# Attention and spectral mixing in one kernel: values loaded in fp32 by SyncE, and their bf16 copies shared by GpSimd and VectorE

## The chip, the core and the metric

The kernel runs on one core of a Trainium2 chip. The time is what the device needs for one execution of the whole program, in microseconds. Sixteen runs of the kernel before took 455.35 to 459.65 us, with a median of 456.8 us. The engines are named as in the profile: PE is TensorE (matrix products), DVE is VectorE, ACT is ScalarE, POOL is GpSimd, SP is SyncE, which here only starts transfers. GpSimd starts transfers too, and only its transfers convert fp32 to bf16 on the way.

## The reference

Two operations follow one another. The first is causal attention in a window of 128 positions with a linear bias, for 8 batches, 8 heads, 576 positions and 64 channels a head; the second multiplies the lowest 64 Fourier modes of the sequence by complex matrices of 512 x 512 each.

```python
scores = scale * np.matmul(q, k.transpose(0, 1, 3, 2))
bias = slopes[:, None, None] * (-np.abs(rel))[None, :, :]
mask = (rel >= 0) & (rel < 128)
attn = softmax(np.where(mask, scores + bias[None], -1e9))
x = np.matmul(attn, v).transpose(0, 2, 1, 3).reshape(B, S, H * D)

X = np.fft.rfft(x, axis=1)
Yr = einsum('bmd,mde->bme', Xr, w_r) - einsum('bmd,mde->bme', Xi, w_i)
Yi = einsum('bmd,mde->bme', Xr, w_i) + einsum('bmd,mde->bme', Xi, w_r)
y = np.fft.irfft(Y, n=S, axis=1)          # Y is 0 above mode 64
u = x + y
return u + np.maximum(u @ w_ch, 0.0)
```

All inputs are fp32 in memory. The mode matrices are the bulk: 128 of them (64 real, 64 imaginary) of 1.05 MB each, of which the imaginary one of mode 0 isn't needed.

## The kernel before

**Attention** works on 16 units, a unit being one batch and four heads. The order of all work is written by hand: the list `STAGE` names some 23 steps with a lag each, and stage s runs each step for unit s minus its lag, so that loads, casts, transposes, scores, exponentials, products with the values and normalisation of several units are under way at once. An engine runs its own instructions strictly in the order in which this list issues them; so does each queue of transfers.

For a unit, `load` brings queries (one transfer, 2304-byte runs), keys (per pair of heads a main part of 512 positions and a tail of 64, both tails into the lower 64 partitions, `L230`) and values (main `L216` and tail `L220`). Queries and keys are started by SyncE as fp32. Values are started by GpSimd and arrive as bf16. Every raw buffer is double: `cast` of unit u ends with `load` of unit u+2 into the same place, which waits for the cast.

`cast` turns raw data into what TensorE takes. For q and k it is one VectorE instruction that converts to bf16 and interleaves the heads (`L259`). For v it is eight instructions, one for each of four quarters of 32 partitions (n) and each of two alternating positions (a): quarter (n, a) goes to the 32 partitions that start at 64 (n % 2) + 32 a of the buffer `vb` (`L252`), beside columns of ones from which the row sums come; a ninth copies the tail into `vt` (`L255`). The eight wait until the value products of unit u-2 have left the same `vb` buffer. In a stage VectorE's order is: values of unit s, keys of unit s+2, `norm` (reciprocal and product, `L380`, `L381`) of unit s-1's first two heads, queries of unit s+3, two mask products (`L339`), `norm` of the other two heads. `value` (`L365`) writes one PSUM buffer, so the second product of a unit waits for the first `norm`.

Key tails of both head pairs lie in partitions 0 to 63, and two transposes of 64 rows handle them (`L282`); the unused upper half is set to zero once (`L500`).

**Weights before their time.** While attention runs, GpSimd starts some mode matrices as bf16: `AHEAD` says how many after which stage, into a pool of `EARLY` tiles, and a one-element copy (`gate`, `L562`) from the first normalised result of the unit before holds each back to its stage. `LATER` does the same into raw buffers that attention no longer needs (the list `spare`). GpSimd's queue is thus, in each stage: values of unit s+2 (two transfers), gate, one weight.

**Spectral part.** After attention TensorE multiplies mode after mode (`L870`); weights that were not brought early stream in as fp32, started by SyncE, into six tiles (`NWA`) in the space that attention leaves, and eight more (`AGAIN`) as bf16 into early tiles that have been used. Projections, inverse transform and output follow from there.

Of the kernel before, what the change touches and what calls it, by code (L numbers as in the profile page):

```python
# [10 lines left out]
FP32 = mybir.dt.float32  # L11
BF16 = mybir.dt.bfloat16
# [8 lines left out]
P = 128  # L21
D = 64
# [5 lines left out]
FULL = 4  # L28
TAIL = 64

TPP = 9

W = D + 2

NC = 24


STAGE = (
# [68 lines left out]
class _Attention:  # L107
# [100 lines left out]
    def load(self, w, u):  # L208
        nc = self.nc
        if u >= len(self.units):  # L210
            return
        b, g = self.units[u]
        hs = slice(4 * g, 4 * g + 4)
        if w == "v":
            t = self.raw["v"][:, u % 2], self.raw["t"][64:96, u % 2]
            nc.gpsimd.dma_start(  # L216
                out=t[0],
                in_=self.v[b, hs, : FULL * P].rearrange("h (p j) d -> p h (j d)", j=4),
            )
            nc.gpsimd.dma_start(  # L220
                out=t[1],
                in_=self.v[b, hs, FULL * P :].rearrange("h (p j) d -> p h (j d)", j=2),
            )
        elif w == "k":
            t = self.raw[w][:, u % 2]
            for e in range(2):
                src = self.k[b, 4 * g + 2 * e : 4 * g + 2 * e + 2]
                for row, j0, n, part in ((slice(0, P), 0, 8, src[:, : FULL * P]),
                                         (slice(0, 64), 8, 2, src[:, FULL * P :])):
                    nc.sync.dma_start(  # L230
                        out=t[row, e, j0 : j0 + n].rearrange("p j d -> p (j d)"),
                        in_=part.rearrange("h (p j) d -> p h (j d)", j=n),
                    )
        else:
            t = self.raw[w][:, u % 2]
            nc.sync.dma_start(
                out=t.rearrange("p e j d -> p e (j d)"),
                in_=self.q[b, hs].rearrange("(e h) (p j) d -> (h p) e (j d)", h=2, j=TPP),
            )
        self.loaded[w, u] = t  # L240

    def cast(self, u, w):

        nc = self.nc
        src = self.loaded.pop((w, u))
        if w == "v":
            rows = src[0].rearrange("p h (j a d) -> p h j a d", j=2, a=2)
            for n in range(4):
                c0 = W * (n % 2)
                for a in range(2):  # L250
                    r = 64 * (n % 2) + 32 * a
                    nc.vector.tensor_copy(  # L252
                        self.vb[u % 2][r : r + 32, n // 2, :, :, c0 : c0 + D],
                        rows[32 * n : 32 * n + 32, :, :, a])
            nc.vector.tensor_copy(self.vt[u % 2][64:96, :, :, :D],  # L255
                                  src[1].rearrange("p h (j d) -> p h j d", j=2))
        else:
            dst = self.mid.tile([P, src.shape[2], 2, D], BF16, tag=w, name=w)
            nc.vector.tensor_copy(dst.rearrange("p j e d -> p e j d"), src)  # L259
            self.casted[u, w] = dst  # L260
        self.load(w, u + 2)

    def transpose(self, u, w):
        nc = self.nc
        src = self.casted.pop((u, w))
        tag = dict(tag="sc", bufs=2) if (u, w) == (0, "k") else dict(tag="tp")
        tp = self.ps.tile([P, TPP * P], BF16, name="tp", **tag)
        self.open[w, u] = tp
        if w == "q":
            for j in range(TPP):  # L270
                nc.tensor.transpose(tp[:, j * P : (j + 1) * P],
                                    src[:, j].rearrange("p e d -> p (e d)"), self.ident)
            return
        main = tp[:, : FULL * 2 * P].rearrange(
            "d (h j b a i p) -> d j a i h b p", h=2, j=2, b=FULL, a=2, p=16, i=2)
        rest = tp[:, FULL * 2 * P :].rearrange("d (j h i p) -> d j h i p", j=2, h=2, i=2)
        for j in range(8):
            nc.tensor.transpose(
                main[:, j // 2 % 2, j % 2, j // 4], src[:, j].rearrange("p e d -> p (e d)"),
                self.ident.rearrange("k (b p h) -> k h b p", b=FULL, h=2))  # L280
        for j in range(2):
            nc.tensor.transpose(  # L282
                rest[:, j], src[:64, 8 + j].rearrange("p e d -> p (e d)"),
                self.ident[:64, :64].rearrange("k (p i h) -> k h i p", i=2, h=2))

    def evacuate(self, u, w):
        tp = self.open.pop((w, u))
# [123 lines left out]
    def channels(self, u, _):  # L411
# [3 lines left out]
        if g < self.NG - 1:  # L415
            return
        xt = self.open.pop(("xt", u))
        NM = self.F.shape[2] // 2
        view = self.XC[:, : 4 * NC * NM].rearrange(
            "p (q s t b m) -> p q t s b m", q=2, s=3, t=2, b=8)[:, :, :, :, b]  # L420
# [13 lines left out]
def kernel(  # L434
# [10 lines left out]
    nc = tc.nc  # L445
    ctx.enter_context(tc.manual_schedule(engines=ALL | {SP}))
    B, H, S, _ = q.shape
    NM, DM, _ = moe_w_r.shape
    AHEAD = {0: 1, 1: 1, 2: 1, 3: 1, 4: 1, 5: 1, 7: 1, 8: 1, 9: 1, 10: 1, 11: 1, 12: 1, 13: 3}
    LATER = {14: 3, 15: 2}  # L450
    EARLY, NWA, NWB, AGAIN = 15, 6, 2, 8
    HM = NM // 2

    const = ctx.enter_context(tc.tile_pool(name="const", bufs=1))
    x = const.tile([P, B, FULL + 1, DM], BF16, name="x")
    XC = const.tile([P, 4 * NC * NM + 16 * NM], BF16, name="XC")
    ident = const.tile([P, P], BF16, name="ident")
# [7 lines left out]
        tc.tile_pool(name="w1", bufs=EARLY, side="right", reuse_waits="tile")  # L465
    )
    rawpool = actx1.enter_context(tc.tile_pool(name="raw", bufs=1, side="right"))
    raw = {w: rawpool.tile([P, 2, 2, n, D], FP32, name=w + "r") for w, n in (("q", TPP), ("k", 10))}
    raw["v"] = rawpool.tile([P, 2, 4, 4 * D], BF16, name="vr")
    raw["t"] = rawpool.tile([P, 2, 4, 2 * D], BF16, name="vtr")  # L470
    spare = [raw[w][:, i].rearrange("p e j d -> p (e j d)") for w in "qk" for i in range(2)]
    spare = [t[:, : 2 * DM].bitcast(BF16) for t in spare]
    spare.append(raw["v"].rearrange("p u h d -> p (u h d)"))
    spare = [t.rearrange("p (a e) -> p a e", a=4) for t in spare]
    wq, homes, todo_w, again = {}, {}, [0, *range(2, 2 * NM)], []

    def load_w(n, pool, bf16, chosen=None):


        for i in ([i for i in todo_w if i not in again][:n] if chosen is None else chosen):  # L480
            todo_w.remove(i)
            src = (moe_w_r, moe_w_i)[i % 2][i // 2].rearrange("(p a) e -> p a e", a=4)
            homes[i] = pool
            if bf16:
                t = spare.pop(0) if pool is None else pool.tile([P, 4, DM], BF16, tag="w", name="w")
                nc.gpsimd.dma_start(out=t, in_=src)
                wq[i] = [t[:, a] for a in range(4)]
            else:
                t = pool.tile([P, 4, DM], FP32, tag="w", name="w")
                for part in ((slice(0, 4),) if i < 2 * NM - 1  # L490
                             else (slice(0, 2), slice(2, 3), slice(3, 4))):
                    nc.sync.dma_start(out=t[:, part], in_=src[:, part])
                wq[i] = [t[:, a].bitcast(BF16)[:, 1::2] for a in range(4)]

    with ExitStack() as actx:
        at = _Attention(tc, actx, q, k, v, (ident, F, FT), x, XC, raw)
        n = len(at.units)
        for w, u in (("q", 0), ("k", 0), ("q", 1), ("k", 1)):
            at.load(w, u)
        nc.vector.memset(raw["k"][64:, :, :, 8:], 0.0)  # L500
        done = set()

        def run(name, arg, u):
            if 0 <= u < n and (name, arg, u) not in done:
                done.add((name, arg, u))
                getattr(at, name)(u, arg)
# [10 lines left out]
        for t in at.kT:  # L517
            nc.vector.memset(t[:, 2 * S :], 0.0)
        at.distances(pool)
        at.load("v", 0)  # L520
        at.fixtures(0)
        next(table, None)
        at.load("v", 1)
        at.fixtures(1)
        nc.gpsimd.memset(XC[:, 4 * NC * NM :], 0.0)
        run("cast", "q", 0)
# [23 lines left out]
        for stage in range(min(lags), n + max(lags)):  # L550
            for name, arg, lag in STAGE:
                run(name, arg, stage - lag)
                if name in ("transpose", "exp") and side.get(stage):
                    for _ in range(1 + (name == "transpose")):
                        fn, h = side[stage].pop(0)
                        fn(h)
            if stage == 3:
                at.inverse_table()
            if stage in AHEAD:
                if stage:  # L560
                    b, g = at.units[stage - 1]
                    nc.gpsimd.tensor_copy(gate[:1, :1], x[:1, b, 0, 256 * g : 256 * g + 1])  # L562
                load_w(AHEAD[stage], early, True)
            if stage in LATER:
                load_w(LATER[stage], None, True)

    with ExitStack() as mctx:
# [273 lines left out]
        for g in range(NM // 4):  # L841
# [5 lines left out]
            for i in range(8):  # L847
# [3 lines left out]
                w = wq[2 * m + ri]  # L851
# [13 lines left out]
                for a in range(4):  # L865
                    c0 = (a // 2 * 2 * NC + 16 * (1 - ri) + a % 2 * 8) * NM + m
                    window.append(XC[:, c0 : c0 + 31 * NM + 1 : NM])
# [9 lines left out]
                k = 8 * g + i  # L877
# [4 lines left out]
                if k == K1 - 1:  # L882
# [15 lines left out]
                    for b in range(2):  # L898
                        nc.gpsimd.dma_start(
                            out=FM.rearrange("(k v) b s -> k v b s", v=16)[:, b, b],  # L900
# [103 lines left out]
```

The softmax here doesn't subtract the row's maximum and nothing guards it: scores larger than these inputs give would overflow.

## Time and profile before

| | |
|---|---|
| median of 16 runs | 456.8 us (455.35 to 459.65) |
| the profiled execution | 458.43 us, of which the span from first to last instruction 456.5 us |
| mean granted TensorE clock | 0.890 |
| busy: PE, DVE, ACT, POOL | 366.7, 192.6, 152.9, 102.9 us |
| transfers from SyncE's queue | 132.17 MB, 73.0% of 16 engines' span |
| transfers from GpSimd's queue | 20.17 MB (as written), 26.2% |
| read from memory, written to it | 162.53 MB, 9.44 MB |
| first and last exponential of attention | 11.5 us, 136.9 us |
| first product with a mode's weights | 145.56 us |
| value copies on VectorE (`L252`) | 128, median 284 ns, at most 1058 ns |

In the profile a line such as `L252 DVE COPY vb<-vr 32x512 bf16<-32x512 bf16 x8` names the source line, the engine, the operation, what is written from what, the shapes (partitions x elements) and how many there were. In a listing in order of time, the first two numbers are the start and the length in us, and a bracket at the end says how long the engine had stood idle before, and for whom. Transfer rates in GB/s count bytes as they are written, so a transfer that converts fp32 to bf16 counts half of what it reads.

### The profile page before, as it was taken

Reading aid. Unit: us, or ns where it says so; the run is one execution under the profiler, and the core shown is the slowest. Engines: PE = TensorE matmul, PEld = TensorE weight load, DVE = VectorE, ACT = ScalarE, POOL = GpSimd, SP = SyncE. Lnnn points to the kernel's source line nnn. Section 1 sums busy time; section 2 is a strip of 40 time slices with the busy share of each in tenths; the row PEclk is TensorE's granted clock in tenths of the full one; section 3 lists DMA queues with packets and bytes.
Section 4 is the critical chain, followed back from the end, with each engine's and each line's share of the span. In section 5 each row is a group of like instructions: output and inputs, shape, how many; then the busy total and the mean of one; then the engine's idle time right before and its main releaser. Section 6 shows DMA issues by size and latency. Waiting matters only on the chain. (4 is left out here: it accounts for less than half of the span.)

```text
span 456.5 us, 8161 instructions
## 1 busy us (share of the span) xinstructions
PE 366.7 (80%) x3330; PEld 192.6 (42%) x3330; DVE 192.6 (42%) x420; ACT 152.9 (33%) x196; POOL 102.9 (23%) x170
## 2 busy tenths in 40 slices
PE   4588898899996876567665776999999999776994
PEld 3256576766664431222222233444444443332331
DVE  6889889999994210010101023121212112220584
ACT  4758798888881000000000011112111210110772
POOL 8943323242521300200000000000000000054781
PEclk8659899999998885775667699999999999999998
DMA  7999999999899999999999999999999999997598
GB/s 261 206 252 265 269 227 238 241 269 278 131 192 275 316 315 314 327 373 427 419 420 423 422 422 419 420 420 419 422 420 419 423 417 421 420 406 247 188 351 300
DMA packets 47625, 152.85 MB, mean 335 GB/s; under 512 B 7252, under 2 KB 18276, under 8 KB 35044
## 3 DMA queue, kind: packets, MB, share of 16 engines
q1 hardware_dynamic: 31156, 132.17, 73.0%
q0 software_dynamic: 16432, 20.17, 26.2%
q8 instruction: 26, 0.43, 0.4%
q14 instruction: 11, 0.09, 0.1%
HBM read 162.53 MB, written 9.44 MB: 377 GB/s over the span
## 5 line engine op out<-in xcount | busy, mean ns | idle before, releaser
L870 PE MATMUL acc<-w,XC 128*32 128x512 bf16 x464 | 136.4, 458 | 47.3 <-DMA w<-in_moe_w_r_dram 28.0
L870 PEld LDWEIGHTS <-XC 128*32 128x32 bf16 x508 | 60.2, 140 | 124.0 <-issue 88.0
L329 ACT ACTIVATE att<-sc 128x1024 bf16<-128x1024 f32 x64 | 64.0, 1031 | 8.3 <-PE sc L320 8.3
L655 POOL DMA_DIRECT2D Z<-yq x19 | 9.7, 518 | 215.2 <-issue 208.6
L642 ACT CAST ZW<-zw 128x512 bf16<-128x512 f32 x8 | 4.7, 585 | 157.5 <-PE zw L640 157.5
L614 DVE TENSOR_SCALAR yq<-acc 128x512 bf16<-128x512 f32 x13 | 9.0, 689 | 97.0 <-PE acc L870 96.9
L365 PE MATMUL av<-vb,att 128*128 128x132 bf16 (+1 forms) x576 | 38.7, 218 | 9.6 <-DVE x L381 6.8
L717 ACT CAST XW<-my 128x512 bf16<-128x512 f32 x36 | 19.3, 589 | 75.5 <-PE my L665 75.5
L365 PEld LDWEIGHTS <-att 128*128 128x128 bf16 x704 | 36.9, 99 | 15.5 <-DVE x L381 11.7
L689 DVE COPY xT<-tr 128x1024 bf16<-128x1024 bf16 x18 | 12.5, 692 | 69.8 <-PE tr L687 69.8
L252 DVE COPY vb<-vr 32x512 bf16<-32x512 bf16 x128 | 38.1, 298 | 2.3 <-DMA vr<-in_v_dram 0.8
L708 PE MATMUL my<-wch,xT 128*64 128x512 bf16 x288 | 34.5, 382 | 0.8 <-DVE xT L689 0.8
L216 POOL DMA_DIRECT2D vr<-in_v_dram x16 | 17.9, 1118 | 60.3 <-DVE vb L252 60.3
L320 PE MATMUL sc<-qT,kT 64*64 64x256 bf16 (+2 forms) x640 | 25.7, 269 | 3.0 <-ACT kT L289 2.4
L381 DVE TENSOR_TENSOR x<-av,rec 128x640 bf16<-128x640 f32 x32 | 26.4, 825 | 1.1
L822 DVE TENSOR_TENSOR o<-yy,r 128x512 f32<-128x512 f32 (+1 forms) x24 | 21.7, 953 | 6.4 <-ACT r L779 4.7
L320 PEld LDWEIGHTS <-kT 64*64 64x64 bf16 x640 | 14.8, 111 | 20.5 <-issue 16.4
L708 PEld LDWEIGHTS <-xT 128*64 128x64 bf16 x288 | 14.8, 109 | 18.9 <-issue 6.9
L307 PE MATMUL sc<-bias,ident 128*128 128x512 bf16 x64 | 20.9, 411 | 1.2 <-ACT att L329 1.0
L644 DVE CAST Z<-z 64x512 bf16<-64x512 f32 x16 | 11.0, 689 | 23.7 <-PE z L637 23.6
L779 ACT ACTIVATE r<-mm 128x512 f32<-128x512 f32 (+1 forms) x24 | 18.1, 812 | 7.5 <-PE mm L665 4.2
L339 DVE TENSOR_TENSOR att<-att,mask 128x1024 bf16<-128x1024 bf16 x32 | 20.6, 684 | 0.0
(140 smaller groups left out, 414.5 us busy)
## 6 DMA issues: line engine op xcount, KB each, us to landing
w<-in_moe_w_r_dram SPq DMA_DIRECT2D x53, 1024.0 KB, 18.4
w<-in_moe_w_i_dram SPq DMA_DIRECT2D x45, 1024.0 KB, 18.1
qr<-in_q_dram SPq DMA_DIRECT2D x16, 576.0 KB, 8.3
kr<-in_k_dram SPq DMA_DIRECT2D x32, 256.0 KB, 6.1
w<-in_moe_w_i_dram POOLq DMA_DIRECT2D x15, 512.0 KB, 12.0
out_dram<-o SPq DMA_DIRECT2D x10, 512.0 KB, 3.7
vr<-in_v_dram POOLq DMA_DIRECT2D x16, 256.0 KB, 6.8
w<-in_moe_w_r_dram POOLq DMA_DIRECT2D x8, 512.0 KB, 8.8
```

Of the source, the lines that this page charges most:

```text
L252: nc.vector.tensor_copy(self.vb[u % 2][r : r + 32, n // 2, :, :, c0 : c0 + D], rows[32 * n : 32 * n + 32, :, :, a])
L307: nc.tensor.matmul(sc[:, e], lhsT=self.ident, rhs=self.bias[self.units[u][1]][:, 2 * e + h].rearrange("p j n -> p (j n)"), start=True, sto ...
L320: nc.tensor.matmul(sc[64 * half : 64 * half + 64, e, j * 256 + c0 : j * 256 + c0 + n], lhsT=kT[row, k0 : k0 + 64], rhs=qT[row, h, q0 : q0 ...
L329: self.nc.scalar.activation(self.att[u % 2][:, kt * 8 * P : (kt + 1) * 8 * P], sc.rearrange("p e n -> p (e n)"), AF.Exp, scale=1.0 / math. ...
L339: nc.vector.tensor_tensor(out=rows, in0=rows, in1=self.table[g][:, t % 2 :: 2], op=ALU.mult)
L365: nc.tensor.matmul(bank[:, qt * W : qt * W + rhs[j].shape[1]], lhsT=att[:, o : o + P], rhs=rhs[j], start=(n == 0 and j == 0), stop=(n == l ...
L381: nc.vector.tensor_tensor(out=self.x[:, b, :, cs].rearrange("p t (h d) -> p h t d", h=2), in0=tiles[:, :, :, :D], in1=rec.unsqueeze(-1).br ...
L708: nc.tensor.matmul(mm[ROWS[half]], lhsT=lhsT, rhs=wch[:, dt], start=(dt == 0), stop=False, skip_group_check=True,)
L717: nc.scalar.copy(XW[:, j, n], mms[n])
L779: nc.scalar.activation(r[:, c], mm[:, c], AF.Relu)
L822: nc.vector.tensor_tensor(out=o[:, c], in0=yy[:, c], in1=r[:, c], op=ALU.add)
L870: nc.tensor.matmul(into[32 * (i // 2) : 32 * (i // 2) + 32], lhsT=window[a], rhs=w[a], start=(ri == 0 and a == 0), stop=(ri == (m > 0) and ...
```

## The change

Values are loaded by SyncE instead of GpSimd, as fp32: the raw buffers for values double in size, each read being 1 KB (tail: 512 bytes). The conversion to bf16 thus moves into `cast`: of the eight shifted quarter copies the first five (in the order of the loops) are made by GpSimd, three and the tail by VectorE. The values of the first two units are requested right after the queries and keys of the first two units, ahead of the tables' setup.

The raw key buffer is laid out anew: both head pairs' main parts first, then 128 columns for the tails, the tail of the first pair in partitions 0 to 63 and that of the second in 64 to 127. The key cast becomes two instructions, the tail transposes four instead of two, and the setting to zero goes.

The memory for this comes from the early weights: `EARLY` is 14 instead of 15 and stage 3 asks for none. In return there are seven spare raw buffers instead of five, and `LATER` fills four instead of two in stage 15.

```diff
+NPOOL = 5
...
         if w == "v":
             t = self.raw["v"][:, u % 2], self.raw["t"][64:96, u % 2]
-            nc.gpsimd.dma_start(
+            nc.sync.dma_start(
                 out=t[0],
                 in_=self.v[b, hs, : FULL * P].rearrange("h (p j) d -> p h (j d)", j=4),
             )
-            nc.gpsimd.dma_start(
+            nc.sync.dma_start(
                 out=t[1],
...
-                for row, j0, n, part in ((slice(0, P), 0, 8, src[:, : FULL * P]),
-                                         (slice(0, 64), 8, 2, src[:, FULL * P :])):
+                for row, c0, n, part in ((slice(0, P), 512 * e, 8, src[:, : FULL * P]),
+                                         (slice(64 * e, 64 * e + 64), 1024, 2,
+                                          src[:, FULL * P :])):
...
-                    nc.vector.tensor_copy(
+                    (nc.gpsimd if 2 * n + a < NPOOL else nc.vector).tensor_copy(
                         self.vb[u % 2][r : r + 32, n // 2, :, :, c0 : c0 + D],
                         rows[32 * n : 32 * n + 32, :, :, a])
...
-            dst = self.mid.tile([P, src.shape[2], 2, D], BF16, tag=w, name=w)
-            nc.vector.tensor_copy(dst.rearrange("p j e d -> p e j d"), src)
+            dst = self.mid.tile([P, TPP, 2, D], BF16, tag=w, name=w)
+            if w == "q":
+                nc.vector.tensor_copy(dst.rearrange("p j e d -> p e j d"), src)
+            else:
+                nc.vector.tensor_copy(dst[:, :8].rearrange("p j e d -> p e j d"),
+                                      src[:, : 16 * D].rearrange("p (e j d) -> p e j d", e=2, j=8))
+                nc.vector.tensor_copy(dst[:, 8].rearrange("p e d -> p (e d)"), src[:, 16 * D :])
...
         for j in range(2):
-            nc.tensor.transpose(
-                rest[:, j], src[:64, 8 + j].rearrange("p e d -> p (e d)"),
-                self.ident[:64, :64].rearrange("k (p i h) -> k h i p", i=2, h=2))
+            for e in range(2):
+                row = slice(64 * e, 64 * e + 64)
+                nc.tensor.transpose(
+                    rest[row, j], src[row, 8, j],
+                    self.ident[row, row].rearrange("k (p i h) -> k h i p", i=2, h=2))
...
-    AHEAD = {0: 1, 1: 1, 2: 1, 3: 1, 4: 1, 5: 1, 7: 1, 8: 1, 9: 1, 10: 1, 11: 1, 12: 1, 13: 3}
-    LATER = {14: 3, 15: 2}
-    EARLY, NWA, NWB, AGAIN = 15, 6, 2, 8
+    AHEAD = {0: 1, 1: 1, 2: 1, 4: 1, 5: 1, 7: 1, 8: 1, 9: 1, 10: 1, 11: 1, 12: 1, 13: 3}
+    LATER = {14: 3, 15: 4}
+    EARLY, NWA, NWB, AGAIN = 14, 6, 2, 8
...
-    raw["v"] = rawpool.tile([P, 2, 4, 4 * D], BF16, name="vr")
-    raw["t"] = rawpool.tile([P, 2, 4, 2 * D], BF16, name="vtr")
+    raw["v"] = rawpool.tile([P, 2, 4, 4 * D], FP32, name="vr")
+    raw["t"] = rawpool.tile([P, 2, 4, 2 * D], FP32, name="vtr")
...
-        for w, u in (("q", 0), ("k", 0), ("q", 1), ("k", 1)):
+        for w, u in (("q", 0), ("k", 0), ("q", 1), ("k", 1), ("v", 0), ("v", 1)):
             at.load(w, u)
-        nc.vector.memset(raw["k"][64:, :, :, 8:], 0.0)
...
         at.distances(pool)
-        at.load("v", 0)
         at.fixtures(0)
         next(table, None)
-        at.load("v", 1)
         at.fixtures(1)
```

More of the change, by code (lines that the diff above doesn't have):

```diff
@@ L227, in load @@
                 src = self.k[b, 4 * g + 2 * e : 4 * g + 2 * e + 2]
-                for row, j0, n, part in ((slice(0, P), 0, 8, src[:, : FULL * P]),
-                                         (slice(0, 64), 8, 2, src[:, FULL * P :])):
+                for row, c0, n, part in ((slice(0, P), 512 * e, 8, src[:, : FULL * P]),
+                                         (slice(64 * e, 64 * e + 64), 1024, 2,
+                                          src[:, FULL * P :])):
                     nc.sync.dma_start(
-                        out=t[row, e, j0 : j0 + n].rearrange("p j d -> p (j d)"),
+                        out=t[row, c0 : c0 + n * D],
                         in_=part.rearrange("h (p j) d -> p h (j d)", j=n),
@@ L467 @@
     rawpool = actx1.enter_context(tc.tile_pool(name="raw", bufs=1, side="right"))
-    raw = {w: rawpool.tile([P, 2, 2, n, D], FP32, name=w + "r") for w, n in (("q", TPP), ("k", 10))}
-    raw["v"] = rawpool.tile([P, 2, 4, 4 * D], BF16, name="vr")
-    raw["t"] = rawpool.tile([P, 2, 4, 2 * D], BF16, name="vtr")
[L471 to L474, printed above, removed]
+    raw = {"q": rawpool.tile([P, 2, 2, TPP, D], FP32, name="qr"),
+           "k": rawpool.tile([P, 2, 2 * TPP * D], FP32, name="kr")}
+    raw["v"] = rawpool.tile([P, 2, 4, 4 * D], FP32, name="vr")
+    raw["t"] = rawpool.tile([P, 2, 4, 2 * D], FP32, name="vtr")
+    spare = [raw["q"][:, i].rearrange("p e j d -> p (e j d)") for i in range(2)]
+    spare += [raw["k"][:, i] for i in range(2)]
+    spare += [raw["v"][:, i].rearrange("p h d -> p (h d)") for i in range(2)]
+    spare.append(raw["t"].rearrange("p u h d -> p (u h d)"))
+    spare = [t[:, : 2 * DM].bitcast(BF16).rearrange("p (a e) -> p a e", a=4) for t in spare]
     wq, homes, todo_w, again = {}, {}, [0, *range(2, 2 * NM)], []
```

## The prediction

> **What bounds the kernel now.** I read the table of busy slices first, then sums over three stretches, then one stage of VectorE in order of time.
>
> ```profile
> DVE  6889889999994210010101023121212112220584
> DMA  7999999999899999999999999999999999997598
> GB/s 261 206 252 265 269 227 238 241 269 278 131 192 275 316 315 314 327 373 427 419 420 423 422 422 419 420 420 419 422 420 419 423 417 421 420 406 247 188 351 300
> ```
>
> One slice is 11.4 us. VectorE is full in the first twelve slices (attention) and nearly idle after; from slice 18 on the DMA engines move a steady 420 GB/s of fp32 weights. So the kernel has two halves with different bounds.
>
> ```profile
> core 0: us, PE busy (x) PEld busy (x) DVE busy (x) ACT busy (x) POOL busy (x), PEclk, DMA share, GB/s
> 30.00:124.00 94.00, 84.46 (x1472) 62.53 (x1470) 87.65 (x209) 79.84 (x88) 33.54 (x49) 0.97 1.07 244
> 124.00:140.00 16.00, 14.01 (x253) 10.67 (x251) 13.37 (x34) 11.69 (x14) 4.42 (x9) 1.00 1.06 192
> 140.00:400.00 260.00, 209.18 (x1170) 92.83 (x1168) 42.48 (x97) 23.98 (x45) 8.88 (x20) 0.86 1.02 397
> ```
>
> In 30 to 124 us VectorE works 87.65 of 94 us, TensorE 84.46, ScalarE 79.84. Bytes are counted as written, and a casting load reads twice what it writes, so 192 GB/s there is not a slack link: at 124 us seven casting weight loads are issued at once, 1.05 MB read each. From then on transfers never pause until the last weights near 417 us: 115 of the 127 weights and w_ch are still to be read, 121.6 MB, and 121.6 MB / 420 GB/s = 289.5 us, so 124 + 289.5 = 413.5 us. The end is therefore set by two things: when that burst starts (behind attention stage 13, so by VectorE's pace) and how many weights are in before it.
>
> One stage of VectorE:
>
> ```profile
> 89.27 2.37 DVE L252 COPY vb<-vr 32x512 bf16<-32x512 bf16 x8
> 91.67 0.28 DVE L255 COPY vt<-vtr 32x512 bf16<-32x512 bf16 x1
> 91.99 0.83 DVE L259 CAST k<-kr 128x1280 bf16<-128x1280 f32 x1
> 92.73 0.21 DVE L380 RECIPROCAL rec<-av 128x10 f32<-128x10 f32 x1
> 92.98 0.82 DVE L381 TENSOR_TENSOR x<-av,rec 128x640 bf16<-128x640 f32 x1
> 93.72 0.75 DVE L259 CAST q<-qr 128x1152 bf16<-128x1152 f32 x1
> 94.39 1.29 DVE L339 TENSOR_TENSOR att<-att,mask 128x1024 bf16<-128x1024 bf16 x2
> 95.59 0.21 DVE L380 RECIPROCAL rec<-av 128x10 f32<-128x10 f32 x1
> 95.84 0.82 DVE L381 TENSOR_TENSOR x<-av,rec 128x640 bf16<-128x640 f32 x1
> ```
>
> No row has idle time in front of it; the next eight copies start at 96.58, so a stage is 7.31 us of gapless VectorE work.
>
> Last, what happens where GpSimd and VectorE work in the same microsecond, at start-up and at one mask (each line is an instruction, start and duration):
>
> ```profile
> 17.84 1.01 POOL L141 MEMSET vb<- 64x1056 bf16 x1
> 17.95 1.05 DVE L252 COPY vb<-vr 32x512 bf16<-32x512 bf16 x1
> ...
> 19.11 1.12 POOL L141 MEMSET vb<- 64x1056 bf16 x1
> 19.32 1.06 DVE L252 COPY vb<-vr 32x512 bf16<-32x512 bf16 x1
> ...
> 123.41 1.28 DVE L339 TENSOR_TENSOR att<-att,mask 128x1024 bf16<-128x1024 bf16 x2
> 123.62 0.51 POOL L562 COPY gate<-x 1x1 bf16<-1x1 bf16 x1 [0.27 <-DVE x L381]
> ```
>
> A copy that takes 0.28 us alone took 1.05 and 1.06 us beside a memset, both times ending 0.15 us after it (18.85 to 19.00, 20.23 to 20.38). In reverse, a one-element GpSimd copy took 0.51 us and ended 0.04 us after the first mask product (123.41 + 0.68, its mean on the page, = 124.09; 123.62 + 0.51 = 124.13). The two engines take turns. The PSUM-to-SBUF copy of queries at 13.19 us took 1.36 us beside memsets and 1.34 us away from them: work that reads PSUM is not held.
>
> **The change, part by part, for one unit of attention.**
>
> VectorE work. Five of eight copies go: start to start they are 2.40/8 = 0.30 us, so -1.50. The three that stay read fp32. The fp32 tensor_scalar rows at start-up (128x320 0.326 us, 128x640 0.497) give 0.53 ns an element and 0.43 us at 512, against 0.284: three times +0.145 = +0.44, and vt +0.145. (The k and q casts, 0.827 at 1280 and 0.750 at 1152, would give 0.37; that is the lower bound, 0.25 us less over four copies.) The k cast becomes 128x1024 (0.70) plus 128x128 (0.22) in place of 0.83: +0.10. Sum -1.50 + 0.44 + 0.145 + 0.10 = -0.82 us a unit if GpSimd were elsewhere.
>
> GpSimd work. A 64x512 bf16 copy at 8.66 us, with no lock in the way, took 0.603 us, 64x384 took 0.505: I take 0.60 for a 32x512 one. No row has GpSimd reading fp32 at this width or writing to other partitions than it reads, which several of these copies do; the dearest near row is the select of 32x256 from fp32 at 0.613, so 1.2 us at 512 is the upper bound; 0.5 (the 384 row) the lower. I take 0.60, for the operation is the same, a copy. Five are 3.0 us of a 7 us stage; the two load issues that leave its queue (1.18 + 0.56 us) were no load on VectorE. GpSimd itself has room: the price is the turns.
>
> The turns. The copies of unit u+1 are freed when value(u-1, 1) ends, since that unit's vb buffer is then free. That product starts after norm 0 and ends at 95.35 us in the stage shown, 0.24 us before the second reciprocal. So two GpSimd copies fit beside reciprocal and norm 1 (PSUM work, 1.0 us, free). Copies 3, 4 and 5 meet VectorE's next work: its own three vb copies and vt. A blocked VectorE copy ends 0.15 us after its blocker at 512 bf16, where it needs some 0.13 us of streaming, so its fixed part is hidden; an fp32 one needs 0.27. A blocked GpSimd operation lost only 0.05 us of its own (memset 1.12 us, of which 0.20 waiting, against 0.97). One pair is then 0.55 + 0.27 = 0.82 us where VectorE alone needs 0.44: +0.38, three times +1.14 us.
>
> By row, -0.82 + 1.14 = +0.32 us a unit. Units 0 to 13 lie ahead of the burst: 14 x 0.32 = +4.5 us.
>
> The Trainium skill ("SBUF — State Buffer", section "SBUF: two separate sides") says that the pair of ports which VectorE and GpSimd share is an exclusive lock, held for the whole instruction. The rows above agree on who waits, but not on the price: with whole instructions in line a pair would cost 0.60 + 0.43 = 1.03 us, +0.59 a pair, +0.95 us a unit and +13 us in place of +4.5. I keep to the rows.
>
> Weights before the burst. The first list loses its stage 3 entry, 12 to 11 weights by stage 12, the pool goes from 15 to 14 tiles; the two spares more are filled inside the saturated stretch. One weight of 1.05 MB joins the 289.5 us: +2.5 us. Its place in the attention stretch is not a bottleneck that gains from its absence, for VectorE sets the pace there.
>
> At nothing I cost: the value loads on the wire (same bytes read; 0.29 MB more written in 7.7 us, 38 GB/s on 244, below 420); SyncE's two more issues a unit, between a weight's 0.35 and a key load's 0.78 us (four in 3.12), so at most 1.6 on 3.7 us of a 7.3 us stage; the two more key transposes (two took 0.27 us; TensorE has 9.5 idle of 94 us, and uncovered they would cost 14 x 0.27 = 3.8); the kr memset (0.48 us at 0.91, before the first data).
>
> New waits. On SyncE, the load of v(u+2) waits for the slower engine's copies of v(u), with k(u+4) and q(u+5) queued behind; VectorE's vt ends last in the turns above, so it adds nothing in a steady stage. At start-up, q of unit 4 was issued near 21.8 us and would come behind v2 near 24 us; with 8.3 us to landing it arrives near 33 us, where it is cast at 30.7: up to 1.5 us. The memsets move up by the 2.1 us of two load issues and meet the bias products; against that the 0.77 us wait for v0 and two blocked copies (0.77 each) go. Start-up: 0, bounds -1.5 and +1.5.
>
> Sum: +4.5 + 2.5 + 0 = +7.0 us. The profiled execution took 458.43 us (span 456.5), 1.6 above the median of 456.8; the change is set on the median: 463.8 us.
>
> **Rivals.**
>
> A. GpSimd's copies are longer. At 0.85 us, VectorE's first copy waits 0.45 us and three pairs cost +0.63 each: 2.3 in place of 1.14, +1.5 a unit, 14 x 1.5 + 2.5 = +23, 480 us. At the bound of 1.2 us it is +3.3 a unit, 505 us. For it: fp32 in, other partitions out, no row. Against: the same operation at 0.60.
>
> B. Faster: the turns cost little, because GpSimd's copies fall beside PSUM work or VectorE's gaps. It decides from below 0.64 us a unit, for (0.82 - 0.64) x 14 = 2.5. With one collision left (0.38): -0.44 x 14 + 2.5 = -3.7, 453 us; with none -9, 448 us, and there TensorE (84.46 of 94 us, 6.9 us a stage) is the next bound, equal to 7.72 - 0.82. For it: norm and reciprocal are 2 us of each stage. Against: the copies are freed just ahead of VectorE's own.
>
> C. No change: the turns cost near 0.64 us, and the two halves cancel.
>
> **How the numbers follow.** Forecast 0.47 (its own range 460 to 469, one pair more or less, start-up's bounds with it), A 0.24, B 0.22, C 0.07. A measurement of this kernel tells about 0.2%, 0.9 us. Slower 0.71, same 0.07, faster 0.22. For 8 in 10 I leave out A above 480 (about 0.13) and B below 451 (0.05): 451 to 480.
>
> **What would show it.** Right: VectorE's fp32 vb copies at 0.43 us or, blocked, 0.7 to 0.85; stages near 7.6 us; GpSimd copies of 0.6 to 0.9 us; the first of the clustered weight loads at 127 to 129 us rather than 124; 420 GB/s after it as before. Wrong: GpSimd copies over 0.85 us alone (A); VectorE's copies unblocked and stages under 7.1 us (B); or value products waiting for GpSimd's copies, or VectorE idle before q or k casts for late loads, which I hold for absent.

## The result, and the profile after

The changed kernel takes 462.49 us (median of 9 runs, 461.45 to 465.16) against 456.49 us for the kernel before (48 runs by then): a ratio of 1.013, with a 95% interval of 1.0109 to 1.0151, or +5.9 us. The forecast was +7.0 us and 463.8 us. The profiled execution took 462.23 us, its span 460.2 us; that of the kernel before lay about 2 us above its median, so the two spans stand only 3.7 us apart, and below whole kernels are compared by ratios, profiles only by stages.

Part of those 2 us can be seen in the profile of the kernel before: the granted TensorE clock falls to half (0.50, third from the end), and VectorE stands idle for a product of TensorE.

```profile
54.00:56.00 2.00, 2.00 (x23) 1.29 (x22) 2.00 (x4) 0.89 (x1) 1.06 (x2) 0.50 1.10 331
```
```profile
58.26 0.22 DVE L380 RECIPROCAL rec<-av 128x10 f32<-128x10 f32 x1 [1.71 <-PE av L365]
```

The other profiles have such stretches too, at other times; over the first 47 us the mean granted clock is 0.85 in the changed kernel. Comparisons of single profiles outside the steady stages are therefore rough.

The busy slices and the sums over three stretches of the changed kernel:

```profile
DVE  6888999999995210000101033121212122220594
DMA  8879999999899999999999999999999999997498
GB/s 258 257 240 310 286 279 265 277 288 301 205 197 262 318 315 317 315 336 387 424 422 420 422 419 422 419 422 419 422 419 419 421 420 422 419 408 269 169 352 310
```
```profile
30.00:124.00 94.00, 81.77 (x1468) 61.50 (x1458) 88.11 (x159) 77.38 (x85) 54.03 (x80) 0.98 1.01 284
124.00:140.00 16.00, 15.01 (x269) 11.02 (x269) 14.98 (x27) 13.75 (x17) 12.57 (x21) 1.00 0.91 190
140.00:400.00 260.00, 205.90 (x1181) 92.52 (x1177) 43.22 (x99) 23.81 (x45) 8.75 (x20) 0.87 1.02 391
```

The picture is the same: VectorE full in attention (88.11 of 94 us, with 159 instructions where there were 209), then transfers at 420 GB/s. Values in fp32 raised what is written in attention from 244 to 284 GB/s, and from 20 us on no VectorE instruction waits for a value load. GpSimd went from 33.5 to 54.0 us.

One stage of VectorE, in order of time:

```profile
98.94 1.92 DVE L256 CAST vb<-vr 32x512 bf16<-32x512 f32 x3
100.89 0.71 DVE L259 CAST vt<-vtr 32x512 bf16<-32x512 f32 x1
101.63 0.69 DVE L266 CAST k<-kr 128x1024 bf16<-128x1024 f32 x1
102.24 0.22 DVE L268 CAST k<-kr 128x128 bf16<-128x128 f32 x1
102.38 0.21 DVE L391 RECIPROCAL rec<-av 128x10 f32<-128x10 f32 x1
102.62 0.82 DVE L392 TENSOR_TENSOR x<-av,rec 128x640 bf16<-128x640 f32 x1
103.37 0.75 DVE L264 CAST q<-qr 128x1152 bf16<-128x1152 f32 x1
104.03 1.29 DVE L350 TENSOR_TENSOR att<-att,mask 128x1024 bf16<-128x1024 bf16 x2
105.23 0.22 DVE L391 RECIPROCAL rec<-av 128x10 f32<-128x10 f32 x1
105.48 0.82 DVE L392 TENSOR_TENSOR x<-av,rec 128x640 bf16<-128x640 f32 x1
106.34 0.42 DVE L256 CAST vb<-vr 32x512 bf16<-32x512 f32 x1
```

The stage is 7.40 us (98.94 to 106.34) and again without a gap. Three copies and vt take 2.69 us of it, where nine took 2.72 us before. Why four are now as dear as nine were stands in the same microseconds of both engines:

```profile
98.43 0.60 POOL L256 CAST vb<-vr 32x512 bf16<-32x512 f32 x1
98.94 0.42 DVE L256 CAST vb<-vr 32x512 bf16<-32x512 f32 x1
99.07 0.75 POOL L256 CAST vb<-vr 32x512 bf16<-32x512 f32 x1
99.37 0.74 DVE L256 CAST vb<-vr 32x512 bf16<-32x512 f32 x1
99.87 0.71 POOL L256 CAST vb<-vr 32x512 bf16<-32x512 f32 x1
100.12 0.74 DVE L256 CAST vb<-vr 32x512 bf16<-32x512 f32 x1
100.63 0.69 POOL L256 CAST vb<-vr 32x512 bf16<-32x512 f32 x1
```

The copy at 98.43, beside a norm that reads PSUM, takes GpSimd 0.60 us, and VectorE's first takes 0.42: neither was held. From there they take turns, one of each every 0.75 us. Over all units the page has a mean of 666 ns for VectorE's copies and 738 for GpSimd's:

```profile
L256 POOL CAST vb<-vr 32x512 bf16<-32x512 f32 x80 | 59.1, 738 | 15.6 <-issue 10.1
...
L256 DVE CAST vb<-vr 32x512 bf16<-32x512 f32 x48 | 31.9, 666 | 0.9
```

As the measure of a stage I take the start of the vt copy, unit 5 to unit 13, eight stages: before 61.98 to 121.36 us, 7.42 us a stage; after 63.37 to 123.80, 7.55 us. The burst of weight loads starts at 126.65 us instead of 124.09.

### The profile page after: what moved, and what is told of

Its sections match the earlier page's. It is cut to its first block, busy times and chain, and to the rows that moved or that the text cites. A ratio compares the mean times of both kernels' runs of the same rounds, so it can differ in the third digit from the quotient of the medians.

```text
span 460.2 us, 8284 instructions
## 1 busy us (share of the span) xinstructions
PE 365.4 (79%) x3362; PEld 193.5 (42%) x3362; DVE 197.0 (43%) x355; ACT 152.7 (33%) x196; POOL 134.0 (29%) x218
## 5 line engine op out<-in xcount | busy, mean ns | idle before, releaser
L880 PE MATMUL acc<-w,XC 128*32 128x512 bf16 x456 | 131.7, 451 | 45.1 <-DMA w<-in_moe_w_r_dram 26.2
L256 POOL CAST vb<-vr 32x512 bf16<-32x512 f32 x80 | 59.1, 738 | 15.6 <-issue 10.1
L256 DVE CAST vb<-vr 32x512 bf16<-32x512 f32 x48 | 31.9, 666 | 0.9
L350 DVE TENSOR_TENSOR att<-att,mask 128x1024 bf16<-128x1024 bf16 x32 | 22.2, 735 | 0.0
```

The lines of the kernel that those rows point to most:

```text
L256: (nc.gpsimd if 2 * n + a < NPOOL else nc.vector).tensor_copy(self.vb[u % 2][r : r + 32, n // 2, :, :, c0 : c0 + D], rows[32 * n : 32 * n ...
L350: nc.vector.tensor_tensor(out=rows, in0=rows, in1=self.table[g][:, t % 2 :: 2], op=ALU.mult)
L880: nc.tensor.matmul(into[32 * (i // 2) : 32 * (i // 2) + 32], lhsT=window[a], rhs=w[a], start=(ri == 0 and a == 0), stop=(ri == (m > 0) and ...
```

## The experiments

Times below are ratios to runs of the kernel before on the same chip; "steady stage" is the measure just named.

**The turns taken away.** GpSimd's five copies are left out from the third unit on; later units find the values of the first two in those rows.

```diff
                 for a in range(2):
+                    if u >= 2 and 2 * n + a < NPOOL:
+                        continue
                     r = 64 * (n % 2) + 32 * a
```

> The changed kernel with GpSimd's five copies left out from the third unit on (those units use the values of the first two in these rows, so the output is not the reference's). If the turns cost VectorE about 0.95 us a unit: stage 7.45 - 0.95 = 6.5, below TensorE's 6.9, so -0.55 x 12 = -6.6 us, 456 us, and every VectorE value copy at 0.42 us. If the loss lies elsewhere (transfers, start-up, the early weight): 462 us, no change.

Measured: 455.21 us, ratio 0.996 (0.9937 to 0.9982); steady stage 6.97 us. VectorE's stage and the sums over 60 to 116 us, of this kernel and then of the changed one (columns: PE, PEld, DVE, ACT, POOL busy):

```profile
93.28 0.82 DVE L394 TENSOR_TENSOR x<-av,rec 128x640 bf16<-128x640 f32 x1
94.14 1.29 DVE L258 CAST vb<-vr 32x512 bf16<-32x512 f32 x3
95.46 0.42 DVE L261 CAST vt<-vtr 32x512 bf16<-32x512 f32 x1
```
```profile
60.00:116.00 56.00, 52.08 (x953) 40.31 (x958) 51.50 (x107) 51.42 (x58) 7.30 (x14) 1.00 1.05 299
```
```profile
60.00:116.00 56.00, 49.70 (x891) 37.37 (x891) 54.27 (x98) 48.01 (x54) 34.90 (x52) 1.00 1.02 280
```

Three copies and vt now take 1.74 us (94.14 to 95.88) instead of 2.66 (98.94 to 101.60): the turns cost VectorE 0.92 us a stage. Of that, 0.58 us come out at the end of a stage, for now TensorE is the fuller engine (52.08 of 56 us, VectorE 51.50), and VectorE waits 4.2 us for value products between 62 and 122 us, against 0.3 us in the changed kernel. The theory that the loss lay in transfers, start-up and weights alone falls.

**How many copies GpSimd should have.** `NPOOL` 0, 2 and 8 instead of 5, nothing else.

```diff
-NPOOL = 5
+NPOOL = 0      # and 2, and 8
```

> The changed kernel with all eight value copies on VectorE (fp32 in), none on GpSimd. If VectorE paces attention and GpSimd's share relieves it by turns: eight copies of 0.43 us and vt 0.44 are 3.9 us a unit where the changed kernel's three copies and vt take some 2.65 (1.92 + 0.72), so +1.2 us a unit, 14 units ahead of the weight burst: +17 us on 462.5, 479 us. If the loss came from transfers or weights alone and VectorE had room: 462 us, no change.

> The changed kernel with two of eight copies on GpSimd. If only copies that meet VectorE's SBUF work cost a turn, the two fall beside reciprocal and norm and are free: six VectorE copies unblocked at 0.43 us and vt 0.44 are 3.0 us, +0.36 us a unit against the changed kernel, 467.5 us. If every GpSimd copy costs VectorE a turn of about 0.3 us wherever it stands: near 476 us.

> The changed kernel with all eight copies on GpSimd. By the turns VectorE needs 7.45 - 2.65 + 0.44 + 3 x 0.32 = 6.2 us a unit, so TensorE (6.9) or GpSimd's own queue (8 x 0.75 + 0.57 + 0.53 = 7.1 us) sets the pace: 7.1, -0.35 x 14 = -5, 457 us. If late copies hold the value products, or the weight gates behind them slip: slower than the changed kernel, 465 us and more.

| GpSimd's copies | time, us | ratio (95% interval) | steady stage, us |
|---|---|---|---|
| 0 | 473.21 | 1.0354 (1.0324 to 1.0383) | 8.70 |
| 2 | 463.35 | 1.0150 (1.0120 to 1.0179) | 7.90 |
| 5 | 462.49 | 1.0130 (1.0109 to 1.0151) | 7.55 |
| 8 | 467.64 | 1.0230 (1.0198 to 1.0263) | 7.26 |

The steady stages of none and two come out as expected: +1.15 us for none (expected +1.2), +0.35 for two (+0.36). With eight VectorE's stage is 7.26 us (7.1 expected). The first two copies take 0.80 us off a stage, close to two whole VectorE copies: they are free. The next three take off 0.35 us together, 0.12 each.

All three totals were expected wrongly: 479, 467.5 and 457 us. For none the reason is the start. Four units in, at the vt copy of unit 3, the kernels with none and with five copies stand both at 47.2 us, with the same mean clock of 0.85; five copies had gained nothing yet where four steady stages would have gained 4.6. With two, unit 3 stands at 45.5 us, but in that profile the clock was full all along, so how much of its miss lies in the start stays open. With eight, the waits of the first 45 us and one VectorE stage further on show what more copies cost:

```profile
DVE q L264 <- DMA qr<-in_q_dram: 5.4, 1, 5.4
```
```profile
97.28 0.82 DVE L392 TENSOR_TENSOR x<-av,rec 128x640 bf16<-128x640 f32 x1
98.02 0.94 DVE L264 CAST q<-qr 128x1152 bf16<-128x1152 f32 x1
98.88 2.12 DVE L350 TENSOR_TENSOR att<-att,mask 128x1024 bf16<-128x1024 bf16 x2
```

One query cast waits 5.4 us for its load, which stood in SyncE's queue behind a value load that waited for eight GpSimd copies; and the two mask products, 1.29 us undisturbed, take 2.12 us beside GpSimd's copies. Most of the loss stands in GpSimd's queue, in which the gate and the weight request of a stage stand behind the copies. This is stage 13 with eight copies, and then with five:

```profile
124.11 6.42 POOL L256 CAST vb<-vr 32x512 bf16<-32x512 f32 x8
130.60 0.18 POOL L572 COPY gate<-x 1x1 bf16<-1x1 bf16 x1
130.72 0.53 POOL L499 DMA_DIRECT2D w<-in_moe_w_r_dram  x1
```
```profile
126.20 0.51 POOL L572 COPY gate<-x 1x1 bf16<-1x1 bf16 x1 [2.72 <-DVE x L392]
126.65 0.53 POOL L499 DMA_DIRECT2D w<-in_moe_w_r_dram  x1
```

With five, GpSimd stands idle for VectorE before the gate; with eight, the gate waits for the copies. GpSimd's copies are held too (a mean of 746 ns, 0.60 us alone), so its queue needs 7.55 us a stage (requests at 70.35 us in stage 5 and 130.72 in stage 13), no less than with five (66.29 and 126.65). The shorter VectorE stage therefore never reached the weights, and the 4.1 us by which the burst is late were lost before stage 5. So the expected 457 us became 467.64, by the second way that was on record: weight gates that slip.

**The late query load.** In the changed kernel the wait that the prediction bounded at 1.5 us is there; SyncE issues the queries of unit 4 at 25.31 us, behind unit 2's values (before: 21.82):

```profile
24.30 0.37 SPq L219 DMA_DIRECT2D vr<-in_v_dram  x1
...
25.31 0.39 SPq L240 DMA_DIRECT2D qr<-in_q_dram  x1
...
33.30 0.95 DVE L264 CAST q<-qr 128x1152 bf16<-128x1152 f32 x1 [1.47 <-DMA qr<-in_q_dram]
```

The experiment issues that value load after the query loads of units 4 and 5.

```diff
+        if (w, u) == ("v", 0):
+            return
         self.load(w, u + 2)
+        if (w, u) == ("q", 3):
+            self.load("v", 2)
```

> The changed kernel with the load of unit 2's values issued behind the loads that unit 3's query cast frees, so that the queries of unit 4 do not queue behind GpSimd's first copies. If that wait (1.5 us of VectorE idle before a query cast in the changed kernel's profile) lies on the path: -1.5 us, 461.0 us. If later waits swallow it: 462.5 us.

Measured: 461.07 us, 1.0107 (1.0085 to 1.0128). The cast starts at 31.80 us, with no wait, and the burst at 124.9 instead of 126.65 us. The ratio falls by 0.0023, 1.0 us (1.5 expected); the two intervals overlap, so by the times alone neither size nor sign is sure. That the wait is gone is shown by the profile.

**The weight that is not fetched early.** The kernel before with 14 early tiles and no request after stage 3.

```diff
-    AHEAD = {0: 1, 1: 1, 2: 1, 3: 1, 4: 1,
+    AHEAD = {0: 1, 1: 1, 2: 1, 4: 1,
...
-    EARLY, NWA, NWB, AGAIN = 15, 6, 2, 8
+    EARLY, NWA, NWB, AGAIN = 14, 6, 2, 8
```

> The kernel before with only the early weights changed: 14 tiles, none asked for after stage 3. If transfers are saturated from the burst on, one weight of 1.05 MB at 420 GB/s comes on top: +2.5 us, 459.0 us. If its place in attention was no gain, or the stages speed up without it: 456.5 us.

Measured: 458.64 us, ratio 1.0053 (1.0030 to 1.0076), +2.4 us; steady stage 7.42 us, as before. That agrees with the plain price of 1.05 MB at 420 GB/s (2.5 us); its slot in attention gave nothing back that can be seen.

**The keys alone.** Tails on both halves, two casts, four tail transposes, no zeroing; all else as before.

```diff
-            nc.tensor.transpose(
-                rest[:, j], src[:64, 8 + j].rearrange("p e d -> p (e d)"),
+            for e in range(2):
+                row = slice(64 * e, 64 * e + 64)
+                nc.tensor.transpose(
+                    rest[row, j], src[row, 8, j],
...
-        nc.vector.memset(raw["k"][64:, :, :, 8:], 0.0)
```

> The kernel before with the key part alone: tails on both halves, the cast as two instructions, four tail transposes, no zeroing; values, copies and weights as before. By the rows +0.10 us of VectorE a unit (0.70 + 0.22 for 0.83), 14 units: +1.4 us, 458 us. If the four transposes are on the path too: up to +3.8 more, 462 us. If the smaller raw tile and the balanced tails help: 456 us.

Measured: 457.25 us, ratio 1.0002 (0.9980 to 1.0024). The steady stage is 7.49 us, +0.07 where +0.10 was expected, but nothing arrives in the total; 1 us is inside the interval.

**The split without the rest.** The kernel before, its values bf16 by casting loads, with two, three and five copies on GpSimd, and with two from the third unit on.

```diff
-                    nc.vector.tensor_copy(
+                    (nc.gpsimd if 2 * n + a < NPOOL else nc.vector).tensor_copy(
```

> The kernel before (bf16 values from casting loads) with two of the eight copies on GpSimd. They fall beside reciprocal and norm, so by the turns VectorE saves 2 x 0.30 = 0.60 us a unit; TensorE's 6.9 us a stage stops it at some -0.4: 13 x -0.4 = -5, 451.5 us. If every GpSimd copy costs VectorE as much as it saves: 456.5 us; if GpSimd's value loads now queue behind its copies and come late: slower, 460 us.

> The kernel before with five of the eight copies on GpSimd, values still bf16 by casting loads: the split of the changed kernel without fp32 values, key tails or the missing weight. By the turns: -1.50 us, and three pairs of 0.55 + 0.13 = 0.68 in place of 0.30, +1.14, so -0.36 us a unit, -4 us, 452 us. If the copies' turns alone made the changed kernel slower: 460 us or more.

> The kernel before with three of the eight copies on GpSimd (two were 3 us faster, five 0.6). The third meets VectorE's first copy: it costs a turn of about 0.38 and saves 0.30 us, so 0.1 us a unit back: 454 us, near the run with two. If a third still fits beside norm: 451 us.

> Two of eight copies on GpSimd, but from the third unit on: the first two units' copies stay on VectorE, away from GpSimd's setup. In the run with two, GpSimd's copies of units 0 and 1 meet VectorE's queries and keys at 24 to 29 us (4 turns of some 0.4 us against 4 x 0.30 saved) and unit 2's value load waits behind them: even or 1 us better, 452.5 to 453.5 us. If start-up loses VectorE time by four more copies: 454.5 us.

| GpSimd's copies | time, us | ratio (95% interval) | steady stage, us |
|---|---|---|---|
| 2 | 453.48 | 0.9933 (0.9913 to 0.9953) | 7.14 |
| 3 | 454.05 | 0.9921 (0.9899 to 0.9943) | 7.22 |
| 5 | 456.50 | 0.9987 (0.9968 to 1.0007) | 7.30 |
| 2, from unit 2 on | 454.35 | 0.9925 (0.9906 to 0.9945) | 7.19 |

Two or three copies make the kernel 3 to 3.6 us faster than before; the three ratios can't be told apart, so whether the first two units' copies matter stays open. Three came out as expected (454 us); two were expected at 451.5 and five at 452 us, so more was hoped of both. In the run with two, GpSimd's copies end where VectorE's begin (GpSimd's pair, VectorE's mask and norm, and its first value copy):

```profile
68.67 0.68 DVE L341 TENSOR_TENSOR att<-att,mask 128x1024 bf16<-128x1024 bf16 x1
68.91 0.91 POOL L254 COPY vb<-vr 32x512 bf16<-32x512 bf16 x1 [1.55 <-PE av L367]
...
69.52 0.82 DVE L383 TENSOR_TENSOR x<-av,rec 128x640 bf16<-128x640 f32 x1
69.86 0.61 POOL L254 COPY vb<-vr 32x512 bf16<-32x512 bf16 x1
70.38 0.28 DVE L254 COPY vb<-vr 32x512 bf16<-32x512 bf16 x1
```

GpSimd waits out the mask (0.91 us instead of 0.60), makes its second copy beside the norm, and VectorE's first takes its undisturbed 0.28 us. With five, VectorE's copies are at a mean of 535 ns instead of 298 and most of the saving is gone. VectorE also waits for value products there, 2.3 us with two and 1.1 us with five between 62 and 122 us; how the rest of the hoped-for gain divides between that and the turns was not taken apart. These kernels need no fp32 values and no missing weight; those with two or three beat both kernels of this case.

## Why the prediction was right

The forecast and its sign held, and the mechanism of the turns is the one that was drawn. That the sum comes so near is partly luck: the turns were priced some 2.7 us too high and the start-up 1.0 to 1.5 us too low.

- **VectorE's rows.** fp32 copies take 0.417 us undisturbed (0.43 predicted), the key casts 0.69 and 0.22 (0.70 and 0.22). But the two key casts overlap: from the first to the reciprocal behind them it is 0.75 us (101.63 to 102.38), where one cast took 0.74 (91.99 to 92.73). The +0.10 was nothing. In its place the first value copy starts 0.86 us after the norm does (105.48 to 106.34), where it was 0.74 (95.84 to 96.58), and again 0.86 with GpSimd's copies left out (93.28 to 94.14), so that is no turn. The two errors cancel and -0.82 stands, by luck.
- **GpSimd's copy.** 0.60 us undisturbed, by the row of the bf16 copy; reading fp32 and writing other partitions than it reads cost nothing extra. Rival A falls with it: it needed 0.85 us.
- **The turns.** Two copies free beside reciprocal and norm, three paid: as drawn. A pair took 0.75 us rather than 0.82, so the turns cost 0.92 us a unit instead of 1.14, shown by leaving the copies out. -0.82 + 0.92 = +0.10 us a unit against the +0.32 on record; the stages shown stand 0.09 apart (7.40 less 7.31), the mean of eight 0.13 (7.55 less 7.42). If all 14 units went by that mean, the term was 14 x 0.13 = +1.8 us, not +4.5: the mechanism was right and the price of a pair 0.07 us too high. The shared-port rule of the Trainium skill that was set against the rows ("SBUF — State Buffer", "SBUF: two separate sides"), with whole instructions in line, would have a pair at 1.03 us; the runs have 0.75.
- **The weight.** +2.5 us on record, +2.4 measured alone (1.4 to 3.5). Right.
- **Start-up.** Set at 0 within -1.5 and +1.5. The late query load came at 25.31 us and cost a wait of 1.47 us, at its upper bound; undoing it gave 1.0 us of run time, with the doubt said above. The wait was priced rightly, but the earlier value loads were to pay for it, and they did so only in part: the wait for the first values is gone, while VectorE's first three copies and vt still meet GpSimd's setup and take 3.17 us (17.52 to 20.69) instead of 1.74.
- **Sum.** 1.8 + 2.4 + 1.0 to 1.5 = 5.2 to 5.7 us for a measured 5.9, whose own interval is 5.0 to 6.9. It is a sum of single readings: in the two profiles the bursts stand 2.56 us apart, where the first and third term make 2.8 to 3.3, and the stretches at half clock make single profiles unsure by about as much (one wait of 1.71 us was shown).
- **At nothing.** The value loads' bytes and SyncE's added issues stayed hidden in the steady stage, which is as long as VectorE's rows make it; the key part measured +0.1 us by itself, with 1 us of doubt either way.
- **Rival B** had the right condition, turns below 0.64 us a unit. They are 0.92. The kernels with two and three bf16 copies show what its side looks like.

Left open: the start seems longer by GpSimd's setup and five copies a unit standing in VectorE's way (47.2 us at unit 3 with none and with five alike). That is argued from the traces: no run took the setup apart from the copies.

## What to carry to other kernels

Work given to GpSimd is free here only beside what VectorE does out of PSUM; beside its SBUF copies each copy costs a turn, here some 0.3 us out of 0.43 saved, and the less the copy costs VectorE, the less is left. So count the PSUM work next to the point where GpSimd is set free, and begin with that many copies. With bf16 values two or three were best and five gave nothing; with fp32 values five still shortened the stage (7.55 us against 7.90), though the totals of two and five can't be told apart. Look, too, at what else stands in that queue: with eight copies the weight requests came 4.1 us later. And when a load moves to another queue, look up who stands behind it before the first buffers come free: a load that waits for a slower engine delays the loads of all others.

## What was not expected of the hardware

Mask products, which read two tensors from SBUF, are held by GpSimd's copies as plain copies are: a mean of 969 ns with eight copies on GpSimd, 735 with five, 684 before. GpSimd casts fp32 to bf16, from one group of 32 partitions to another, in the 0.60 us in which it copies bf16 within the same partitions. VectorE's first value copy starts 0.74 us after the start of the norm in front of it in the kernels in which VectorE makes all eight, and 0.86 us in those in which the first of the eight are GpSimd's or left out; no run shows the cause.
